# Linear attention with a swish MLP: batches 0 and 1 by head pair, w_in in eight tiles, w_out in 4 KB runs

## The chip, the cores and the metric

The kernel runs on one core of one Trainium2 chip. The metric is the device time of one execution in microseconds, as the median over runs. A profiled execution gives the trace, in which every instruction has a start and a duration. In it PE is TensorE (matmuls; PEld is its weight loads), DVE is VectorE, ACT is ScalarE, POOL is GpSimd, and SP is the engine that only issues DMAs.

## The reference

Inputs q, k, v are float32 of shape (8 batches, 8 heads, 576 positions, 64). The attention is linear: q is softmaxed over the 64 features, k over the 576 positions, and the products are taken as q (k^T v). The result is the input x of a two-layer MLP with 4608 tokens, d_model 512 and d_ff 2048.

```
q_s = exp(q - max(q, -1));  q_s = q_s / (sum(q_s, -1) + 1e-09)
k_s = exp(k - max(k, 2));   k_s = k_s / (sum(k_s, 2) + 1e-09)
kv  = einsum('bhsd,bhse->bhde', k_s, v)
x   = einsum('bhsd,bhde->bhse', q_s, kv)  ->  (B * S, H * D)
h   = x @ w_in
g   = h * (1.0 / (1.0 + exp(-beta * h)))     # beta: one value per d_ff column
out = g @ w_out
```

## The kernel before

**Chunks.** The tokens are cut into nine chunks: the first 512 positions of each of the eight batches, and one chunk (number 8) of the eight tails of 64 positions. They run in the order 0 to 6, 8, 7. For a chunk c, `x_mm` makes the four transposed tiles xT (128 channels, i.e. a pair of heads, by 512 tokens); `mm_a(c, j)` makes the hidden tile h number j of 16 with four matmuls (one per 128 channels, 128x512 each), then ACT's tanh `th` and a DVE multiply `g`; `mm_b(c, j)` adds tile j into the four PSUM accumulators acc0 to acc3 with four matmuls. A block of four such matmuls takes 0.86 us in the chain of the profile. In the steady state blocks of mm_a and mm_b alternate, mm_b two tiles behind mm_a (LAG = 2).

**Attention of a batch.** `q_exp` (ACT), `q_sum` and `q_mul` (DVE) make the softmaxed q, in two halves of four heads. For batches 0 and 1 `q_pet` transposes it on PE, four 128x128 transposes per head pair into a PSUM tile tp, which an engine then copies to qsT. For k only exp is taken; the sum of exp(k) comes from a column of constants beside v. `kv_mm` multiplies exp(k) by v. `kv_norm` divides on DVE by that column and writes the pair's two 64x64 blocks into the diagonal of kvp, with a reciprocal and two multiplies.

**Batches 0 and 1** (b < NW) are special. Their 576 positions are laid over 64 partitions with 9 per partition (RW = 9), and the two heads of a pair stand one above the other on 128 partitions. In the kernel before, exp(k) goes into a zeroed tile in which each head has its own 64 of 128 columns (`kz_exp`, two instructions of 64 partitions for each pair), so that one 128x128 matmul per position makes both heads.

**Order of the work.** The tile framework is in a manual mode: each engine executes its instructions in the order of the code, and waits are semaphores put in from the tiles that instructions share. The whole beginning (batch 0's attention, chunk 0's MLP, batch 1's attention) is therefore written out by hand. `warm` puts dummy matmuls on PE. From chunk 1 on the function `side` places the next batch's work between the blocks.

**Buffers.** PSUM has tags: h with two buffers, att with two, acc0 to acc3 with one each. Weights come in through a staging ring, tag wo, of four buffers of 1 MB; the loads in 2, out 2, in 3 and out 3 wait until the casts of in 0, out 0, in 1 and out 1 have emptied their buffers. The casts to bf16 (`w_cast`) are on POOL but for one.

**DMA queue.** All loads are issued from SP, in the order of the code, and at most eight are under way: each waits for the one eight before it. In the order before: q of batch 0, its four k pairs, its four v pairs, beta, then the weights in the order in 0, out 0 (first half), in 1, out 0 (second half), out 1, in 2, out 2, in 3, then q of batch 1, half of out 3, its k, the other half of out 3, its v, and q, k, v of batch 2.

Of the kernel before, what the change touches and what calls it, by code (L numbers as in the profile page):

```python
# [17 lines left out]
def kernel(  # L18
# [39 lines left out]
    beta_t = const.tile([P, NJ], F32, name="beta_t")  # L58
    beta_r = const.tile([NJ, P], F32, name="beta_r")
    ident16 = const.tile([NJ, NJ], F32, name="ident16")  # L60
    w_in_b = const.tile([P, KT, FF], BF16, name="w_in_b")
    w_out_b = const.tile([P, NJ, DM], BF16, name="w_out_b")
# [9 lines left out]
    w_in_d = moe_w_in.rearrange("(kt p) f -> p kt f", p=P)  # L72
    w_out_d = moe_w_out.rearrange("(j p) f -> p j f", p=P)

# [4 lines left out]

    def load_q(b, parts=1):  # L80
        t = stage.tile([P, H, R * D], F32, tag="q_st", bufs=2, name=f"q_st{b}")
        src = q[b, :, 0:MAIN, :].rearrange("h (p i) d -> p h (i d)", i=R)
        n = H // parts
        for s in range(parts):
            nc.sync.dma_start(t[:, s * n : (s + 1) * n, :], src[:, s * n : (s + 1) * n, :])  # L85
        q_st[b] = t

# [10 lines left out]

    def load_kv(d, src, b, tag, parts=1):
        t = stage.tile([P, H * (R + 1) * D], F32, tag=tag, bufs=2, name=f"{tag}{b}")  # L100
        if b < NW:
            d[b] = t[:, 0 : HP * RW * D].rearrange("p (j r) -> p j r", j=HP)
            sv = src[b].rearrange("(j e) (p i) d -> (e p) j (i d)", e=2, i=RW)
            n = HP // parts
            for s in range(parts):
                nc.sync.dma_start(d[b][:, s * n : (s + 1) * n, :], sv[:, s * n : (s + 1) * n, :])  # L106
        else:
            d[b] = t[:].rearrange("p (h r) -> p h r", h=H)
            nc.sync.dma_start(
                d[b][:, :, 0 : R * D], src[b, :, 0:MAIN, :].rearrange("h (p i) d -> p h (i d)", i=R)  # L110
            )
            e = b % 2
            nc.sync.dma_start(
                d[b][e * TAIL : (e + 1) * TAIL, :, R * D : R * D + D],
                src[b, :, MAIN:S, :].rearrange("h t d -> t h d"),
            )

    def w_load(kind, blk, half=None):
# [3 lines left out]
        if kind == "in":  # L122
            src = w_in_d[:, :, ds(blk * 512, 512)]
            c = slice(0, 512) if half is None else slice(half * 256, half * 256 + 256)
            nc.sync.dma_start(t[:, :, c], src[:, :, c])
        else:
            src = w_out_d[:, ds(4 * blk, 4), :]
            c = slice(0, 4) if half is None else slice(half * 2, half * 2 + 2)
            nc.sync.dma_start(t[:, c, :], src[:, c, :])  # L129

    def w_cast(kind, blk, half, eng):
        t = wst[kind, blk]
        if kind == "in":
            dst = w_in_b[:, :, ds(blk * 512 + half * 256, 256)]
            src = t[:, :, half * 256 : half * 256 + 256]
        else:
            dst = w_out_b[:, ds(4 * blk + 2 * half, 2), :]
            src = t[:, half * 2 : half * 2 + 2, :]
# [7 lines left out]

    def ek_buf(b, eng=None):
        t = work.tile([P, HP * RW * P], BF16, tag="ek", bufs=2, name=f"ek{b}")
        if b < NW:
            ek[b] = t[:].rearrange("p (j i m) -> p j i m", j=HP, i=RW)  # L150
            eng.memset(t[:].bitcast(F32), 0.0)
        else:
            ek[b] = t[:, 0 : R * H * D].rearrange("p (i h d) -> p i h d", i=R, h=H)

    def kz_exp(b, j, m=1):
        for e in range(2):
            r = slice(e * D, (e + 1) * D)
            nc.scalar.activation(  # L158
                ek[b][r, j : j + m, :, e * D : (e + 1) * D],
                k_st[b][r, j : j + m, :].rearrange("p j (i d) -> p j i d", i=RW),  # L160
                ACTF.Exp,
            )

# [63 lines left out]

    def q_mul(b, s, n=2):
        m = H // n
        h = slice(s * m, (s + 1) * m)  # L230
        nc.vector.tensor_tensor(  # L231
            eq[b][:, :, h, :],
# [24 lines left out]
    def kv_mm(b, jj, n=2, tag="att"):  # L257
        t = ps.tile([P, n, D1 if b < NW or COLT else 2 * D1], F32, tag=tag, bufs=2 if tag == "att" else 1, name=f"kv{b}_{jj}")
        att_of[b, jj] = t
        for jl in range(n):  # L260
            j = n * jj + jl
            if b < NW:
                for i in range(RW):
                    nc.tensor.matmul(  # L264
                        t[:, jl, 0:D1],
                        ek[b][:, j, i, :],
                        va[b][:, j, i, :],
                        start=(i == 0),
                        stop=(i == RW - 1),
                    )  # L270
                continue
# [79 lines left out]
    def mm_a(c, j, kts=None, tag=None):  # L351
# [5 lines left out]
        for kt in kts:  # L357
            nc.tensor.matmul(  # L358
                h[:],
                w_in_b[:, kt, ds(j * P, P)],  # L360
                x_of(c)[:, kt, :],
# [115 lines left out]

    load_q(0, parts=2)
    load_kv(k_st, k, 0, "k_st", parts=4)
    load_kv(v_st, v, 0, "v_st", parts=4)  # L480
    nc.sync.dma_start(beta_r[:], moe_beta.rearrange("(j p) -> j p", p=P))
    w_load("in", 0, 0)
    w_load("in", 0, 1)
    w_load("out", 0, 0)
    w_load("in", 1)
    w_load("out", 0, 1)
    w_load("out", 1)
    w_load("in", 2)
    w_load("out", 2)
    w_load("in", 3)  # L490
    load_q(1, parts=2)
    w_load("out", 3, 0)
    load_kv(k_st, k, 1, "k_st", parts=4)
    w_load("out", 3, 1)
    load_kv(v_st, v, 1, "v_st", parts=2)
    load_q(2)
# [4 lines left out]
    make_identity(nc, identity[:])  # L501
    make_identity(nc, ident16[:])
    ek_buf(0, nc.vector)
    nc.vector.memset(kvp[:, 0 : B - 1], 0.0)
    v_buf(0)
    ek_buf(1, nc.gpsimd)
    v_buf(1)

# [14 lines left out]

    warm(18)
    for s in range(2):
        q_exp(0, s)
        q_sum(0, s)
        q_mul(0, s)
    for s in range(2):
        for j in (2 * s, 2 * s + 1):  # L530
            q_pet(0, j, nc.vector)
        warm(10 if s == 0 else 2)
    for j in range(HP):
        kz_exp(0, j)

    tb = ps.tile([P, 512], F32, tag="h", bufs=2, name="tb")

    def attn0(p):
        if 0 < p < 3:
            warm(1, tag="acc3")  # L540
        if p % 2 == 0:
            vz_cast(0, p, nc.gpsimd)
            vz_cast(0, p + 1, nc.gpsimd)
        kv_mm(0, p, n=1, tag=f"acc{p}")
        kv_norm(0, p, n=1)

    for p in range(HP):
        attn0(p)
        if p == 2:
            w_cast("in", 0, 0, nc.gpsimd)  # L550
        if p >= 1:
            x_mm(0, p - 1, nc.scalar)
        if p == 1:
            nc.tensor.transpose(tb[:, 0:NJ], beta_r[:], ident16[:])
            nc.scalar.copy(beta_t[:], tb[:, 0:NJ])
        if p >= 2:
            for j in range(2):
                mm_a(0, j, [p - 2])
    x_mm(0, HP - 1, nc.scalar)
    for kind, blk in (("in", 0), ("out", 0)):  # L560
        for half in range(2):
            if (kind, half) not in (("in", 0), ("out", 1)):
                w_cast(kind, blk, half, nc.gpsimd)
    for kt in (2, 3):
        for j in range(2):
            mm_a(0, j, [kt])
    w_cast("in", 1, 0, nc.vector)
    w_cast("in", 1, 1, nc.gpsimd)
    w_cast("out", 0, 1, nc.gpsimd)
    mm_a(0, 2)  # L570
    mm_a(0, 3)
    mm_b(0, 0)
    mm_b(0, 1)

    def pool_cast(*what):
        for kind, blk in what:
            for half in range(2):
                w_cast(kind, blk, half, nc.gpsimd)

    def tail_zero(t):  # L580
        nc.gpsimd.memset(vt[t][:], 0.0)
        nc.gpsimd.memset(ekt[t][:], 0.0)
        for e in range(2):
            nc.gpsimd.memset(vt[t][ds(e * TAIL, TAIL), e, :, D:D1], 2.0)

    tail_zero(0)
    pool_cast(("out", 1), ("in", 2), ("out", 2))
    tail_zero(1)
    pool_cast(("in", 3), ("out", 3))

    for u in range(4, NJ):
        if u != 5:
            mm_a(0, u)
        if u == 4:
            mm_a(0, 5)
            mm_b(0, 2)
            continue
        if u == 13:
            for j in (0, 1):
                q_pet(1, j, nc.vector)  # L600
        mm_b(0, u - LAG)
        if u in (10, 11):
            q_exp(1, u - 10)
        if u in (10, 12):
            q_sum(1, (u - 10) // 2)
        if u in (11, 13):
            q_mul(1, (u - 11) // 2)
        if u >= 12:
            kz_exp(1, u - 12)
    vz_cast(1, 0, nc.gpsimd, m=2)  # L610
    vz_cast(1, 2, nc.gpsimd, m=2)
    for j in (2, 3):
        q_pet(1, j, nc.vector)
    mm_b(0, NJ - 2)
    kv_mm(1, 0)
    kv_norm(1, 0)
    warm(2)
    kv_mm(1, 1)
    kv_norm(1, 1)
    mm_b(0, NJ - 1)  # L620
    for j in range(HP):
        x_mm(1, j, nc.scalar if j % 2 == 0 else nc.vector, tag="h" if j < 2 else "att")
    for st in range(R):
        store(0, st)
    for kt in range(KT):
        for j in range(2):
            mm_a(1, j, [kt])
    mm_a(1, 2)
    mm_a(1, 3)
# [86 lines left out]
```

The softmax here doesn't subtract the row's maximum and nothing guards it: scores larger than these inputs give would overflow.

## Time and profile before

| | |
|---|---|
| median of 13 runs | 287.96 us (287.62 to 288.41) |
| the profiled execution | 287.74 us, its span 286.0 us |
| PE busy | 279.3 us (98%) |
| DVE, ACT, POOL busy | 180.4, 162.8, 43.7 us |
| h matmuls (line 358), 128x512 | 576, 379 ns each from start to end |
| acc matmuls (line 399), 128x512 | 560, 379 ns each |
| th on ACT (line 368) / g on DVE (line 370) | 687 / 682 ns each |
| first half of batch 0's q arrives, exp starts | 4.56 us |
| first h matmul | 15.33 us |
| x of chunk 1 / its first h matmul | 47.87 / 48.92 us |

The span runs from the first to the last instruction; the time of the execution is 1.74 us longer. [...] the next one starts 216 ns after it (four in 0.86 us). In the first 48 us the DMA engines are 90% busy or more and move 330 to 400 GB/s; later they have room.

### The profile page before, as it was taken

How to read it: one execution, taken by the hardware profiler on the slowest of the kernel's cores; microseconds unless marked ns; L12 is line 12 of the kernel's file. 1: busy time of each engine (PE TensorE's matmuls, PEld its weight loads, DVE VectorE, ACT ScalarE, POOL GpSimd, SP SyncE). 2: the span in 40 equal slices, each digit the busy share in tenths (PEclk: the TensorE clock that was granted, in tenths of full speed). 3: DMA queues.
4: the chain of work that ended last, by engine and by line, in shares of the span. 5: the costliest groups of instructions: out<-in, count | busy, mean ns of one | idle time of the engine just before them, and what ended most of it. 6: DMA issues, size and time to landing. Idle time of an engine off the chain costs nothing.

```text
span 286.0 us, 4169 instructions
## 1 busy us (share of the span) xinstructions
PE 279.3 (98%) x1611; PEld 129.8 (45%) x1611; DVE 180.4 (63%) x281; ACT 162.8 (57%) x236; POOL 43.7 (15%) x58
## 2 busy tenths in 40 slices
PE   8899999999999999999999999999999999999995
PEld 3444445444444444444444444444445444445543
DVE  7944497695478457854694569546964596455361
ACT  4763586684486448734683468355934564554451
POOL 4458833210030030000300030003000000000000
PEclk9999999999999999999999999999999999999999
DMA  7999999908942963197219912793370033005003
GB/s 231 381 382 388 370 389 326 290 5 247 293 155 65 322 168 143 28 328 202 93 56 252 300 42 109 176 268 109 147 197 25 1 149 73 0 0 149 0 0 147
DMA packets 56371, 50.08 MB, mean 175 GB/s; under 512 B 26256, under 2 KB 48032, under 8 KB 56352
## 3 DMA queue, kind: packets, MB, share of 16 engines
q1 hardware_dynamic: 56208, 49.69, 56.2%
q8 instruction: 12, 0.20, 0.3%
q10 hardware_dynamic: 144, 0.13, 0.1%
q14 instruction: 7, 0.06, 0.1%
HBM read 36.71 MB, written 9.44 MB: 161 GB/s over the span
## 4 chain that ended last, share of the span: by engine, by line
PE 85%; DMA 11%; SPq 1%; POOL 1%; issue 0%; ACT 0%; ACTq 0%
PE h L358 40%; PE acc L399 39%; DMA w_in<-in_moe_w_in_dram 6%; DMA k_st<-in_k_dram 5%; PE x L314 2%; PE kv L276 2%; PE acc L391 1%; POOL w_in_b L145 1%; PE kv L264 0%; PE tp L250 0%; SPq L85 0%; SPq L106 0%; PE x L318 0%; ACT ek L158 0%; SPq L129 0%
## 5 line engine op out<-in xcount | busy, mean ns | idle before, releaser
L368 ACT ACTIVATE th<-h,beta_t 128x512 bf16<-128x512 f32 x144 | 98.6, 687 | 99.0 <-PE h L358 97.2
L370 DVE SCALAR_TENSOR_TENSOR g<-th,h 128x512 bf16<-128x512 bf16 x144 | 97.9, 682 | 88.7 <-ACT th L368 87.3
L358 PE MATMUL h<-xT,w_in_b 128*128 128x512 bf16 x576 | 145.3, 379 | 0.6 <-POOL w_in_b L145 0.3
L399 PE MATMUL acc<-w_out_b,g 128*128 128x512 bf16 x560 | 141.9, 379 | 0.0
L358 PEld LDWEIGHTS <-w_in_b 128*128 128x128 bf16 x576 | 55.3, 98 | 66.3 <-issue 2.7
L399 PEld LDWEIGHTS <-g 128*128 128x128 bf16 x560 | 54.5, 98 | 65.5 <-DVE g L370 0.5
L145 POOL CAST va<-v_st 128x2048 bf16<-128x2048 f32 (+2 forms) x12 | 17.2, 1456 | 144.5 <-DMA v_st<-in_v_dram 144.5
L225 DVE TENSOR_REDUCE rq<-eq 128x16 f32<-128x1024 bf16 x18 | 21.6, 1198 | 2.5 <-ACT eq L214 2.5
L231 DVE TENSOR_TENSOR eq<-eq,rq 128x1024 bf16<-128x1024 bf16 x18 | 22.6, 1254 | 0.1
L214 ACT ACTIVATE eq<-q_st 128x1024 bf16<-128x1024 f32 x16 | 16.3, 1048 | 3.0 <-DMA q_st<-in_q_dram 2.9
L143 ACT CAST xT<-x 128x512 bf16<-128x512 f32 x20 | 11.6, 586 | 10.9 <-PE x L314 10.1
L145 DVE COPY o<-acc 128x512 f32<-128x512 f32 (+1 forms) x19 | 12.1, 670 | 3.4 <-PE acc L399 3.2
L143 ACT COPY o<-acc 128x512 f32<-128x512 f32 (+1 forms) x18 | 9.5, 578 | 5.8 <-PE acc L399 2.9
L169 ACT ACTIVATE ek<-k_st 128x1024 bf16<-128x1024 f32 x12 | 12.6, 1047 | 0.0
L472 PE MATMUL warm<-kvp 128*128 128x512 bf16 x34 | 11.2, 480 | 1.2 <-DVE kvp L500 1.2
L314 PE MATMUL x<-qsT,kvp 128*128 128x512 bf16 x32 | 11.7, 380 | 0.4 <-DVE kvp L309 0.2
L158 ACT ACTIVATE ek<-k_st 64x576 bf16<-64x576 f32 x16 | 10.9, 679 | 0.8 <-DMA k_st<-in_k_dram 0.6
L145 DVE CAST xT<-x 128x512 bf16<-128x512 f32 x16 | 10.9, 684 | 0.5 <-PE x L314 0.5
L145 POOL CAST w_out_b<-w_out 128x1024 bf16<-128x1024 f32 x8 | 8.2, 1042 | 6.7 <-DMA w_out<-in_moe_w_out_dram 6.5
L309 DVE TENSOR_TENSOR kvp<-kv,rk 64x256 bf16<-64x256 f32 (+2 forms) x24 | 8.0, 333 | 0.6
L145 POOL CAST w_in_b<-w_in 128x1024 bf16<-128x1024 f32 x7 | 7.2, 1042 | 3.6 <-DMA w_in<-in_moe_w_in_dram 3.5
L472 PEld LDWEIGHTS <-kvp 128*128 128x128 bf16 x34 | 3.8, 119 | 6.2 <-issue 3.8
(40 smaller groups left out, 75.3 us busy)
## 6 DMA issues: line engine op xcount, KB each, us to landing
out_dram<-o SPq DMA_DIRECT2D x14, 512.0 KB, 3.4
q_st<-in_q_dram SPq DMA_DIRECT2D x6, 1024.0 KB, 6.6
k_st<-in_k_dram SPq DMA_DIRECT2D x6, 1024.0 KB, 9.1
v_st<-in_v_dram SPq DMA_DIRECT2D x6, 1024.0 KB, 10.6
w_in<-in_moe_w_in_dram SPq DMA_DIRECT2D x3, 1024.0 KB, 9.8
k_st<-in_k_dram SPq DMA_DIRECT2D x8, 288.0 KB, 7.6
q_st<-in_q_dram SPq DMA_DIRECT2D x4, 512.0 KB, 7.8
w_out<-in_moe_w_out_dram SPq DMA_DIRECT2D x4, 512.0 KB, 9.5
```

What stands on the lines that cost most here:

```text
L143: eng.copy(dst, src)
L145: eng.tensor_copy(dst, src)
L169: nc.scalar.activation(ek[b][:, :, h, :].rearrange("p i h d -> p h i d"), k_st[b][:, h, 0 : R * D].rearrange("p h (i d) -> p h i d", i=R), ...
L214: nc.scalar.activation(eq[b][:, :, s * m : (s + 1) * m, :].rearrange("p i h d -> p h i d"), q_st[b][:, s * m : (s + 1) * m, :].rearrange(" ...
L225: nc.vector.tensor_reduce(rq[b][:, 0, :, h], eq[b][:, :, h, :], axis=AX.X, op=ALU.add)
L231: nc.vector.tensor_tensor(eq[b][:, :, h, :], eq[b][:, :, h, :], rq[b][:, 1, :, h].unsqueeze(3).to_broadcast((P, R, m, D)), ALU.mult,)
L314: nc.tensor.matmul(t[:], kvp[:, c, j, :], qsT[c][:, :, j, :])
L358: nc.tensor.matmul(h[:], w_in_b[:, kt, ds(j * P, P)], x_of(c)[:, kt, :], start=(kt == 0), stop=(kt == KT - 1),)
L368: nc.scalar.activation(th[:], h[:], ACTF.Tanh, scale=beta_t[:, j : j + 1])
L370: nc.vector.scalar_tensor_tensor(out=g[:], in0=th[:], scalar=1.0, in1=h[:], op0=ALU.add, op1=ALU.mult)
L399: nc.tensor.matmul(acc[st][:], g[:, ds(st * P, P)], w_out_b[:, j, :], start=(j == 0), stop=(j == NJ - 1),)
L472: nc.tensor.matmul(t[:, 0:cols], kvp[:, B - 1, 0, :], kvp[:, B - 1, :, :].rearrange("p j r -> p (j r)")[:, 0:cols],)
```

## The change

- **exp(k) dense.** For batches 0 and 1 exp(k) goes into a tile without zeros, one instruction of 128x576 for each pair. The zeroing of the two ek tiles is gone.
- **kv in quadrants.** Each 128x128 matmul becomes two of 64x64, one for each head, at tile positions (0, 0) and (64, 64).
- **By head pair.** k and v of both batches are loaded pair by pair, k and v in turn. exp, the cast of v, kv_mm and kv_norm run pair by pair too; three of the four qsT copies of batch 0, and one of batch 1's, move to ACT.
- **w_in in eight tiles.** w_in_b becomes eight tiles of 256 columns. Hidden tile j now is every second column of tile j // 2, so a weight load reads with a step of two elements. beta is read as 8 rows of 256 and transposed in two steps to match.
- **w_out in 4 KB runs.** A partition takes two neighbouring rows of w_out (4 KB), where it took rows of 2 KB from different places.
- **Order.** The last weight block (out 3) is loaded behind k and v of batch 1. In chunk 0, mm_b(0, 0..3) stand together, and mm_b(0, 12..15), which use out 3, stand behind x and the first two h tiles of chunk 1. One half of in 1 is cast on ACT instead of DVE.

The core of the diff:

```diff
-    w_in_b = const.tile([P, KT, FF], BF16, name="w_in_b")
+    w_in_b = [const.tile([P, KT, 2 * P], BF16, name=f"w_in_b{hh}") for hh in range(NJ // 2)]
...
-    w_out_d = moe_w_out.rearrange("(j p) f -> p j f", p=P)
+    w_out_d = moe_w_out.rearrange("(hh p e) f -> p hh e f", p=P, e=2)
+    w_in_u = [t[:].rearrange("p kt (q e) -> p kt e q", e=2) for t in w_in_b]
...
+    def kz_exp(b, j):
+        if j == 0:
+            ek_buf(b)
+        nc.scalar.activation(ek[b][:, j, :], k_st[b][:, j, :], ACTF.Exp)
...
+                    for e in range(2):
+                        r = slice(e * D, (e + 1) * D)
+                        nc.tensor.matmul(
+                            t[r, jl, 0:D1],
+                            ek[b][r, j, ds(i * D, D)],
+                            va[b][r, j, i, :],
+                            start=(i == 0),
+                            stop=(i == RW - 1),
+                            tile_position=(e * D, e * D),
+                        )
...
-                w_in_b[:, kt, ds(j * P, P)],
+                w_in_u[j // 2][:, kt, j % 2, :],
...
+    load_q(0, 2)
+    for j in range(HP):
+        load_kv(k_st, k, 0, "k_st", [j])
+        load_kv(v_st, v, 0, "v_st", [j])
     w_load("in", 0, 0)
+    nc.sync.dma_start(beta_r[:], moe_beta.rearrange("(hh q) -> hh q", q=2 * P))
     w_load("in", 0, 1)
     w_load("out", 0, 0)
+    w_load("out", 0, 1)
     w_load("in", 1)
-    w_load("out", 0, 1)
     w_load("out", 1)
     w_load("in", 2)
     w_load("out", 2)
+    load_q(1, 2, 0)
     w_load("in", 3)
...
+    load_q(1, 2, 1)
+    for j in range(HP):
+        load_kv(k_st, k, 1, "k_st", [j])
+        load_kv(v_st, v, 1, "v_st", [j])
+    w_load("out", 3)
...
+    warm(18)
+    q_exp(0, 0)
+    q_sum(0, 0)
+    q_mul(0, 0)
+    q_exp(0, 1)
+    kz_exp(0, 0)
+    vz_cast(0, 0, nc.gpsimd)
+    q_sum(0, 1)
+    q_mul(0, 1)
+    kz_exp(0, 1)
+    vz_cast(0, 1, nc.gpsimd)
+    warm(5)
+    q_pet(0, 0, nc.scalar)
+    q_pet(0, 1, nc.scalar)
+    kv_mm(0, 0, n=1, tag="acc0")
+    kv_norm(0, 0, n=1)
+    warm(3)
+    kv_mm(0, 1, n=1, tag="acc1")
+    kv_norm(0, 1, n=1)
+    kz_exp(0, 2)
+    vz_cast(0, 2, nc.gpsimd)
+    q_pet(0, 2, nc.scalar)
+    q_pet(0, 3, nc.vector)
+    kz_exp(0, 3)
+    vz_cast(0, 3, nc.gpsimd)
+    x_mm(0, 0, nc.scalar, tag="h")
+    warm(1, tag="acc0")
+    kv_mm(0, 2, n=1, tag="acc2")
+    kv_norm(0, 2, n=1)
+    x_mm(0, 1, nc.scalar, tag="h")
+    warm(3, tag="acc1")
+    x_mm(0, 2, nc.scalar)
+    kv_mm(0, 3, n=1, tag="acc3")
+    kv_norm(0, 3, n=1)
...
+    for kt in range(KT):
+        for j in range(2):
+            mm_a(0, j, [kt])
+    mm_a(0, 2)
+    mm_a(0, 3)
+    for j in range(4):
+        mm_b(0, j)
+    w_cast("in", 1, 0, nc.scalar)
...
+    for u in range(6, NJ - 2):
+        mm_a(0, u, tag="att" if u == 6 else None)
+        if u == 9:
+            q_exp(1, 0)
+            q_sum(1, 0)
+        if u == 10:
+            q_mul(1, 0)
+        if u == 12:
+            q_exp(1, 1)
+            q_sum(1, 1)
...
+            q_mul(1, 1)
+            kz_exp(1, 0)
+        mm_b(0, u - 2)
+    q_pet(1, 0, nc.vector)
+    q_pet(1, 1, nc.vector)
+    mm_a(0, NJ - 2)
+    kv_mm(1, 0, n=1)
+    kz_exp(1, 1)
+    mm_a(0, NJ - 1)
+    kv_norm(1, 0, n=1)
+    kv_mm(1, 1, n=1)
+    kv_norm(1, 1, n=1)
+    kz_exp(1, 2)
+    q_pet(1, 2, nc.scalar)
+    q_pet(1, 3, nc.vector)
+    kz_exp(1, 3)
+    x_mm(1, 0, nc.scalar, tag="h")
+    kv_mm(1, 2, n=1)
+    kv_norm(1, 2, n=1)
+    x_mm(1, 1, nc.vector, tag="h")
+    kv_mm(1, 3, n=1)
+    kv_norm(1, 3, n=1)
+    x_mm(1, 2, nc.scalar)
+    x_mm(1, 3, nc.scalar)
     for kt in range(KT):
         for j in range(2):
             mm_a(1, j, [kt])
+    for j in range(NJ - 4, NJ):
+        mm_b(0, j)
+    for st in range(R):
+        store(0, st)
```

In the changed kernel's order of instructions DVE stands thus around batch 1: the second q_sum, g13, the second q_mul, the copies of tp(1,0) and tp(1,1), g14, g15, the norms of pairs 0 and 1, the copy of tp(1,3), the norm of pair 2, the copy of x(1,1), the norm of pair 3.

## The prediction

> **What bounds the kernel now.** The page first: PE is busy 98% of the span and the granted clock is 9 tenths or more in every slice, so outside a few holes nothing but PE time counts (that row does not show everything: the first warm matmuls start 0.43 us apart until 6.7 us, later ones 0.216).
>
> ```profile
> span 286.0 us, 4169 instructions
> PE 279.3 (98%) x1611; PEld 129.8 (45%) x1611; DVE 180.4 (63%) x281; ACT 162.8 (57%) x236; POOL 43.7 (15%) x58
> PE 85%; DMA 11%; SPq 1%; POOL 1%; issue 0%; ACT 0%; ACTq 0%
> ```
>
> The chain that ended last gives 85% to PE and 11% to DMA. Its answer for the first 52 us shows where DMA stands in it: only ahead of 39 us.
>
> ```profile
> 8.91 6.79 DMA w_in<-in_moe_w_in_dram
> ...
> 16.83 10.26 DMA w_in<-in_moe_w_in_dram
> ...
> 28.68 8.94 DMA k_st<-in_k_dram
> ...
> 39.19 0.61 PE tp L250 x8
> ...
> 48.92 3.29 PE h L358 x14
> ```
>
> From 48.92 on, PE is dense to the end. So the change, which touches only batches 0 and 1, is worth what it does to one moment: when the third h tile of chunk 1 starts (mm_a(1,2)). Before, 8 matmuls at 0.216 us (four in 0.86, chain) follow 48.92, so that is **50.65 us**. The timeline of that stretch has the holes and the durations for the sum:
>
> ```profile
> 37.17 1.88 DVE L231 TENSOR_TENSOR eq<-eq,rq 128x1024 bf16<-128x1024 bf16 x1
> ...
> 39.19 0.61 PE L250 MATMUL tp<-identity,eq 128*128 128x128 bf16 x8 [0.70 <-ACT ek L158]
> ...
> 41.52 0.74 DVE L145 COPY qsT<-tp 128x512 bf16<-128x512 bf16 x2
> ...
> 45.42 0.74 PE L264 MATMUL kv<-va,ek 128*128 128x65 bf16 x18
> ...
> 47.01 1.02 PE L399 MATMUL acc<-w_out_b,g 128*128 128x512 bf16 x4
> ```
>
> The copies of the transposes start 1.7 us after these end, and PE does not notice: in between it has mm_b and mm_a blocks.
>
> [...] the multiply above took 1.88 us, the other multiplies that I looked up 1.21 to 1.23; it began 0.25 us after a POOL cast (36.92 to 37.96). [...] about 0.1 us on each side of the 64-column kv block at 66.39 to 67.03. [...]
>
> **Start, to h(0,2) (before: 18.04 + 2 x 0.216 = 18.47).** Removed at no gain: the ek memsets (DVE 1.98, POOL 2.11); DVE then waits for q's exp until 5.65 anyway, POOL for v until 10.45. exp(k) falls from 8 half-partition instructions in 5.58 us (7.44 to 13.02) to 4 of 0.68 (same free size of 576). Landings, from k0 at 7.40 (1.34 MB asked for up to there) and v0 at 10.40 (2.52 MB): 0.393 MB/us, so v pairs land at 8.15, 9.65, 11.15, 12.65 and k pairs 0.75 earlier. The second q multiply becomes ready at 9.87, POOL holds a v cast from 9.7: I let it lose 0.5 (bounds 0 and 0.66), ending 11.6. On DVE follow norms of pairs 0 and 1 (0.17 + 0.46 each), a qsT copy 0.42, so pair 2's norm ends 14.1, x_mm(0,2) is done 14.4, kv pair 3 starts 14.5, its norm ends 15.65, x_mm(0,3) starts 15.7. Eight h matmuls follow; their xT (ACT 0.59) is done 16.7, in time. h(0,2) starts **17.65** (17.15 without the lock): 0.8 earlier. The two small beta transposes (0.23 each) and beta's DMA lie beside pair 3's norm; fewer warm matmuls (30 for 34) matter only there.
>
> **Chunk 0 up to mm_b(0,11).** DMA takes part of this back. Delivered bytes at a landing exceed the asked-for sum by 0.43 MB up to 20 us, by 0.63 MB from 27 (windows of the DMA rate against the casts). In the new order w_in 1 is at 6.55 MB, lands 21.3; ACT's cast (estimate 1.04, as POOL's) ends 22.4; it is needed six blocks of 0.864 (four matmuls) after 17.65, at 22.84. w_out 1 lands 24.3, cast 25.4, needed three blocks later, 25.43. w_in 2 lands 27.07, cast by 28.16, so mm_a(0,8) starts **28.22** (before 28.83) whether the start gained 0.8 or 1.3. w_out 2 lands 29.8, needed 32.5; w_in 3 lands 34.0, cast 35.1, needed 35.13. Eight blocks of 0.86 later mm_b(0,11) ends at **38.6**. The 4 KB runs may quicken w_out: 1 KB runs moved at 358 GB/s, 2 KB at 388, 2.3 KB at 396; 4 KB could give 0 to 5% on 3.1 MB, 0 to 0.4 us; I take 0. Separate w_in tiles cost nothing: the casts stay 1.04 and are hidden by PE. SP issues 2 more DMAs for v of batch 1 (0.45 each) while MBs are queued ahead; moving w_out 3 behind them brings the last v pair from about 44 to 41.6 and w_out 3 from 41.3 to 44.4, harmless as it is used after 50.
>
> **The hand-over to batch 1 (the loss).** Before, mm_b(0,12..15) stood among transposes, kv and x. Now 16 mm_b matmuls (3.46 us) stand behind x, and these waits have no cover. PSUM tag att has two buffers, which tp0, tp1, kv0, kv1, tp2, tp3, kv2, kv3 take in turn; the changed program's list of waits shows kv(1,0) waiting for the DVE copy of tp(1,0).
> - mm_a(0,12) ends 36.0, th12 (0.69) 36.85, second q exp (1.05) 37.9, reduce (1.21) and reciprocal (0.25) 39.45, g13 (0.68) 40.15, second multiply (1.22, or 0.55 more behind a POOL v cast at 40.05; I take half) 41.65, copy of tp0 (0.42) 42.1. PE has meanwhile done both transposes (0.44) and mm_a(0,14) and stands since 39.93: **2.2 us idle**.
> - kv(1,0) 0.4 with its mode changes, mm_a(0,15) to 43.4, kv(1,1) to 43.8. tp(1,2) needs kv(1,0)'s buffer, freed by its norm, which on DVE stands behind g15: th15 44.3, g15 45.0, norm 45.7. PE starts tp(1,2) at 45.75: **1.95 idle**.
> - From there a serial chain: norm of pair 1 and tp(1,3) 0.9, x(1,0); ACT's copy frees the buffer for kv(1,2), done +1.7; norm, copy of x(1,1) (0.68) and norm of pair 3 on DVE, +3.8; x(1,3) ends +4.05: 49.8. PE has 2.2 us of work in it.
> - 8 h matmuls (1.73) and the 16 postponed mm_b (3.46): mm_a(1,2) at **55.0**. The output copies (ACT 0.59, DVE 0.68, two each) run beside mm_a(1,2), (1,3), 1.73 us: hidden.
>
> Kv in quadrants: 18 matmuls for 9 per pair. The 64-column kv had 40 in 0.64, 16 ns each; if quadrants pair up likewise a pair still takes 0.29, if not 0.58, at most 0.3 x 4 in the hand-over. I take the first.
>
> **Sum.** 55.0 - 50.65 = +4.3 on the profiled execution's 287.74 us (span 286.0 and 1.74 around it): 292.0. The median of 13 is 287.96, 0.2 above that execution, so **292.2**. Bounds: lock costs -0.5/+0.5, w_out's runs -0.4, unpaired quadrants +1.2, my waits 0.5 either way: 290.9 to 294.
>
> **Unknown prices.** A half clock after the two holes: [...] PE works only about a third of 39.9 to 49.8. Lower bound 0 (no hole can gain); upper, the next 16 matmuls at double time, +3.5. I take 0. Weights at step 2 (w_in): loads take 98 ns and start a full matmul ahead, so even doubled they fit into 216 ns: 0; upper bound if some fail to, 10 ns each x 576 = +5.8. [...]
>
> **Rivals.**
> - Main: the waits, 292.2; chance 0.70. For it: the waits are in the program, the durations in the trace. Against: it needs DVE's order to bind at each link.
> - Half clock in the hand-over: 292.2 plus 1 to 3.5, 293.2 to 295.7; 0.10. Against: matmuls kept 0.216 through the thin PE work at 12 to 18 us, though warm matmuls helped there.
> - Strided weights tell: above 295; 0.05.
> - The hand-over costs little and w_out runs help: 288.6 to 290.9; 0.05.
> - **Faster**, the other side: the early exp, v casts and loads of batch 1 keep DVE ahead, and PE stays dense there. From 28.22 the dense work is mm_a(0,8..15) 6.9, mm_b(0,6..15) 8.6, transposes 0.9, kv 1.6, x 0.9, h(1,0..1) 1.7 = 20.6, so 48.85: 1.8 better, 286.2. It decides where the idle of the hand-over (6.1 by my count) stays below 1.8. 0.07, with 286.2 to 287.4. The gain of the start alone, 0.6 at 28.22, is what speaks for it.
> - Within 0.2% (0.58 us, about what a measurement can tell): 0.03.
>
> Slower is 0.70 + 0.10 + 0.05 + 0.05 = 0.90. The range 290.3 to 295.7 holds the main case, the half clock and a little of the milder one, 0.82.
>
> **What would show it.** Right: h(0,2) near 17.6; mm_a(0,8) near 28.2 behind a POOL cast; PE waits of about 2 us ended by a DVE copy of a transpose and by a norm (line 312), x(1,3) near 49.6, then 24 matmuls, and from there the old chain 4 us later. Wrong: no PE hole over 1 us between 39 and 50; matmuls 0.43 apart after it; or h matmuls more than 0.216 apart in later chunks.

## Result and the profile after

The changed kernel takes **293.4 us** in the median (291.38 to 294.24, 11 runs) against 288.02 (48 runs of the kernel before beside it): ratio 1.0171, 95% interval 1.0156 to 1.0187. It is slower, and the range forecast holds it; but it lies 1.2 above the 292.2 that was taken as likeliest, and the reason for that difference is one of the prediction's rivals, the half clock. The profiled execution took 293.72 us, with a span of 291.9 (before: 287.74 and 286.0).

The page of the changed kernel, span and busy line, clock row of the 40 slices, and the chain by engine:

```profile
span 291.9 us, 4299 instructions
PE 282.0 (97%) x1680; PEld 130.5 (45%) x1680; DVE 176.5 (60%) x280; ACT 160.7 (55%) x234; POOL 43.7 (15%) x60
PEclk9999996899999999999999999999999999999999
PE 90%; DVE 5%; ACT 2%; DMA 1%; issue 0%
```

The share of DMA in the chain fell from 11% to 1%, and DVE, which had none worth naming, has 5%. The clock row has two slices, the seventh and eighth (44 to 58 us), where the granted clock is below nine tenths.

The timeline of the hand-over, that is, of the stretch from the last tiles of chunk 0 to the third h tile of chunk 1, in which batch 1's attention is made (start us, duration, engine, line, operation; in brackets the idle time before and who ended it):

```profile
38.50 0.61 PE L250 MATMUL tp<-identity,eq 128*128 128x128 bf16 x8
38.95 1.03 PE L361 MATMUL h<-xT,w_in_b 128*128 128x512 bf16 x4
...
39.75 1.21 DVE L231 TENSOR_TENSOR eq<-eq,rq 128x1024 bf16<-128x1024 bf16 x1
...
40.88 0.75 DVE L150 COPY qsT<-tp 128x512 bf16<-128x512 bf16 x2
...
41.44 0.48 PE L266 MATMUL kv<-va,ek 64*64 64x65 bf16 x18 [1.47 <-DVE qsT L150]
...
43.65 0.69 DVE L373 SCALAR_TENSOR_TENSOR g<-th,h 128x512 bf16<-128x512 bf16 x1 [1.43 <-ACT th L371]
...
44.45 0.46 DVE L312 TENSOR_TENSOR kvp<-kv,rk 64x64 bf16<-64x64 f32 x2
...
44.96 0.40 PE L250 MATMUL tp<-identity,eq 128*128 128x128 bf16 x4 [1.67 <-DVE kvp L312]
...
49.06 0.59 PE L317 MATMUL x<-qsT,kvp 128*128 128x512 bf16 x1 [0.67 <-ACT xT L148]
...
49.44 3.62 PE L361 MATMUL h<-xT,w_in_b 128*128 128x512 bf16 x8
...
52.85 3.88 PE L402 MATMUL acc<-w_out_b,g 128*128 128x512 bf16 x16
...
56.57 1.67 PE L361 MATMUL h<-xT,w_in_b 128*128 128x512 bf16 x7
```

Both holes (idle stretches of PE) are there with the releasers forecast: a copy of a transpose behind the second q multiply, and a norm behind g15. Then come the x matmuls and 24 dense matmuls. mm_a(1,2) starts at 56.57 where it had been 50.65: 5.92 later, and the span is 5.9 longer, so nothing behind it adds to the loss. What was not in the main case stands in the line at 49.44: eight h matmuls take 3.41 us up to 52.85, 0.43 each. The windows of 1 us (busy us of PE, PEld, DVE, ACT, POOL, then granted clock, DMA share, GB/s) show why:

```profile
44.00:45.00 1.00, 0.04 (x1) 0.04 (x2) 0.92 (x5) 0.19 (x1) 1.00 (x2) 1.00 1.10 349
...
46.00:47.00 1.00, 1.00 (x21) 0.47 (x19) 0.68 (x3) 1.00 (x2) 1.00 (x2) 0.77 1.09 348
47.00:48.00 1.00, 1.00 (x20) 0.67 (x19) 0.95 (x3) 0.04 (x1) 0.79 (x4) 0.50 1.18 330
...
52.00:53.00 1.00, 1.00 (x4) 0.45 (x3) 0.00 (x0) 0.33 (x1) 0.00 (x0) 0.50 1.09 250
53.00:54.00 1.00, 1.00 (x6) 0.37 (x5) 0.61 (x2) 0.94 (x2) 0.00 (x0) 0.81 0.25 55
```

The windows from 47 to 53 all have 0.50; 0.77 and 0.81 at the two ends mean that the clock was at half from 46.54 to 53.38, 6.84 us (an estimate: 0.46 and 0.38 of these two windows at 0.50). It is so in some executions only. The 12 executions of the changed kernel, by mean granted clock: seven at 0.988 took 293.4 to 294.24 (mean 293.9), one at 0.994 took 292.3, four at 1.000 took 291.38 to 292.23 (mean 291.8). So the half clock costs 2.1 us, and the median is that of a mixture. Below, "whole clock" means executions at 0.998 or above.

### The profile page after: what moved, and what is told of

It reads as the page before. It is cut to its first block, busy times and chain, and to the rows that moved or that the text cites. A ratio compares the mean times of both kernels' runs of the same rounds, so it can differ in the third digit from the quotient of the medians.

```text
span 291.9 us, 4299 instructions
## 1 busy us (share of the span) xinstructions
PE 282.0 (97%) x1680; PEld 130.5 (45%) x1680; DVE 176.5 (60%) x280; ACT 160.7 (55%) x234; POOL 43.7 (15%) x60
## 4 chain that ended last, share of the span: by engine, by line
PE 90%; DVE 5%; ACT 2%; DMA 1%; issue 0%
PE h L361 42%; PE acc L402 40%; PE x L317 3%; DVE eq L231 2%; DVE rq L225 2%; PE kv L279 2%; DMA q_st<-in_q_dram 1%; PE acc L394 1%; ACT eq L214 1%; DVE g L373 1%; PE kv L266 1%; DVE kvp L312 0%; PE warm L475 0%; DVE rq L226 0%; PE tp L250 0%
## 5 line engine op out<-in xcount | busy, mean ns | idle before, releaser
L150 POOL CAST va<-v_st 128x576 bf16<-128x576 f32 (+1 forms) x14 | 18.1, 1298 | 152.3 <-DMA v_st<-in_v_dram 152.3
L148 ACT CAST xT<-x 128x512 bf16<-128x512 f32 x21 | 12.2, 586 | 9.2 <-PE x L317 8.4
L317 PE MATMUL x<-qsT,kvp 128*128 128x512 bf16 x32 | 12.8, 401 | 1.1 <-ACT xT L148 0.7
L475 PE MATMUL warm<-kvp 128*128 128x512 bf16 x30 | 9.6, 465 | 1.3 <-DVE kvp L505 1.2
L150 DVE CAST xT<-x 128x512 bf16<-128x512 f32 x15 | 10.3, 684 | 0.0
L312 DVE TENSOR_TENSOR kvp<-kv,rk 64x64 bf16<-64x64 f32 (+1 forms) x28 | 8.6, 308 | 0.7
L150 POOL CAST w_in_b<-w_in 128x1024 bf16<-128x1024 f32 (+1 forms) x8 | 8.3, 1060 | 4.1 <-DMA w_in<-in_moe_w_in_dram 4.1
L162 ACT ACTIVATE ek<-k_st 128x576 bf16<-128x576 f32 x8 | 5.4, 680 | 1.1 <-DMA k_st<-in_k_dram 1.1
```

The lines of the kernel that those rows point to most:

```text
L148: eng.copy(dst, src)
L150: eng.tensor_copy(dst, src)
L317: nc.tensor.matmul(t[:], kvp[:, c, j, :], qsT[c][:, :, j, :])
L475: nc.tensor.matmul(t[:, 0:cols], kvp[:, B - 1, 0, :], kvp[:, B - 1, :, :].rearrange("p j r -> p (j r)")[:, 0:cols],)
```

## Experiments

**1. Copies of the first transposes on ACT.** It takes the DVE copies out of the first hole.

```
-    q_pet(1, 0, nc.vector)
-    q_pet(1, 1, nc.vector)
+    q_pet(1, 0, nc.scalar)
+    q_pet(1, 1, nc.scalar)
```

> The copies of tp(1,0) and tp(1,1) go to ACT instead of DVE. Theory (each idle stretch of PE is a wait in a chain of DVE work, and the stretches add up): kv(1,0) no longer stands behind the second q multiply on DVE, so it starts at about 39.8 in place of 41.44; DVE is 0.75 us freer, so kv(1,0)'s norm and with it tp(1,2) come about 1.4 earlier (43.6 in place of 44.96), and everything behind x(1,3) too: 290.4 where the clock stays whole, 292.5 where it halves. Rival 1 (only the second hole counts, since it waits for g15 on DVE whatever kv(1,0) does): the first hole shrinks, tp(1,2) stays within 0.4 of 44.96, and the time stays within 0.5 of the changed kernel's. Rival 2 (ACT is the next bound: its copies push th14 and th15 back): tp(1,2) later than 45.3 and a time above 294.

Measured: 291.7 in the median of 4, ratio 1.0126 (1.0072 to 1.018); by clock 289.74 at 1.000, 290.92 at 0.994, 292.48 and 293.56 at 0.988, so there is one execution at whole clock. Its timeline:

```profile
39.90 0.48 PE L266 MATMUL kv<-va,ek 64*64 64x65 bf16 x18
...
43.41 0.40 PE L250 MATMUL tp<-identity,eq 128*128 128x128 bf16 x4 [1.62 <-DVE kvp L312]
```

kv(1,0) has no hole ahead of it and starts 1.54 earlier, tp(1,2) 1.55 earlier. A hole of 1.62 still stands ahead of tp(1,2), so the first hole was added to the second, not hidden in it. Both rivals fall.

**2. Both first norms ahead of g15.**

```
-    mm_a(0, NJ - 1)
     kv_norm(1, 0, n=1)
     kv_mm(1, 1, n=1)
     kv_norm(1, 1, n=1)
     kz_exp(1, 2)
+    mm_a(0, NJ - 1)
```

> In the hand-over, kv(1,1), the norms of kv(1,0) and kv(1,1) and the exp of pair 2 are issued ahead of mm_a(0,15), so that DVE does both norms before g15. Theory (the second hole is the norm standing behind g15): first hole unchanged (kv(1,0) at 41.4), tp(1,2) at about 43.2 in place of 44.96, x(1,3) 1.4 to 1.7 earlier, 290.2 at whole clock, 292.4 with a half one. Rival (x(1,1) to x(1,3) hang on the DVE chain, which holds the same work in either order): tp(1,2) is early but x(1,3) stays within 0.4 of 49.06, the time within 0.4 of the changed kernel's.

Measured: 290.0, ratio 1.0076 (1.0049 to 1.0103); 289.57, 289.66 and 290.33 at whole clock, 291.39 at 0.992. Its timeline:

```profile
41.45 0.81 PE L266 MATMUL kv<-va,ek 64*64 64x65 bf16 x36 [1.46 <-DVE qsT L150]
42.19 1.04 PE L361 MATMUL h<-xT,w_in_b 128*128 128x512 bf16 x4
43.06 0.88 PE L250 MATMUL tp<-identity,eq 128*128 128x128 bf16 x8
```

The first hole is unchanged and the second is gone: transposes follow mm_a(0,15) at 43.06, with 43.2 expected. So the second hole came from g15 standing ahead of the norm in DVE's order (the norm of pair 0 now starts at 42.34, in the changed kernel at 44.45). The edit also puts mm_a(0,15) behind kv(1,1) on PE, where it runs while DVE does the norms.

**3. Two postponed blocks put into the chain.** mm_b(0,12) ahead of kv(1,3), mm_b(0,13) ahead of x(1,3).

```
     x_mm(1, 1, nc.vector, tag="h")
+    mm_b(0, NJ - 4)
     kv_mm(1, 3, n=1)
     kv_norm(1, 3, n=1)
     x_mm(1, 2, nc.scalar)
+    mm_b(0, NJ - 3)
     x_mm(1, 3, nc.scalar)
...
-    for j in range(NJ - 4, NJ):
+    for j in range(NJ - 2, NJ):
         mm_b(0, j)
```

> Of the four postponed blocks mm_b(0,12..15), 12 goes between x(1,1) and kv(1,3) and 13 between x(1,2) and x(1,3); 14 and 15 stay where they were. Theory (PE has 2.2 us of work in the 4.1 us from tp(1,2) to x(1,3), so postponed work put there costs less than its length): 0.9 to 1.4 us less than the changed kernel, 290.4 to 290.9 at whole clock; the two idle stretches at 40 and 44 stay. PE is also busier in the 6 us ahead of the h block, so if thin work halves the clock, it does so more seldom or for less time. Rival (the chain x(1,1), kv(1,3), x(1,2) has no slack and each block put in delays it by its whole 0.86): the same time as the changed kernel within 0.4. Second rival (w_out's last block, cast late, holds the two blocks up): slower by up to 1.

Measured: 290.56, ratio 1.0079 (1.0053 to 1.0105); two executions at whole clock, both 289.85; 291.27 at 0.994 and 292.26 at 0.988. The gain at whole clock, 291.8 - 289.85 = 1.95, is above the 0.9 to 1.4 expected; the spread of the changed kernel's own times at whole clock (0.85) covers the difference. Two of four executions still lose clock, and the profiled one shows it behind the first hole already, in its windows:

```profile
42.00:43.00 1.00, 1.00 (x20) 0.53 (x15) 0.59 (x1) 0.00 (x0) 0.00 (x0) 0.75 1.08 367
...
49.00:50.00 1.00, 0.85 (x7) 0.32 (x8) 0.69 (x1) 0.00 (x0) 0.00 (x0) 0.83 1.10 234
```

By the same reckoning, from 42.50 to 49.34: again 6.84 us.

**4. Extra matmuls in both holes of PE.** `pad(t, n)` puts n matmuls of 128x512 into tile t.

```
     mm_a(0, NJ - 2)
+    h_of[0, NJ - 1] = ps.tile([P, MAIN], F32, tag="h", bufs=2, name="h0_15")
+    pad(h_of[0, NJ - 1], 6)
     kv_mm(1, 0, n=1)
...
     kz_exp(1, 2)
+    x10 = ps.tile([P, MAIN], F32, tag="h", bufs=2, name="x1_0")
+    pad(x10, 7)
     q_pet(1, 2, nc.scalar)
```

> Extra matmuls, whose results are overwritten, are put into the two idle stretches of PE in the hand-over: six of 128x512 ahead of kv(1,0), seven ahead of tp(1,2). Every wait of the real work stays. Half-clock theory (the matmuls at 0.43 us after x(1,3) come from too little PE work over the 10 us before): all executions show h(1,0..1) in about 1.73 us in place of 3.41 and mm_a(1,2) at about 54.5 in place of 56.57; the times gather at 291.4 to 292.2, like the quicker executions of the changed kernel, and none at 293.4 to 294.3. Rival (the half clock is set off by something else, as a jump in load when dense work comes back): as many executions at 293.4 and above as of the changed kernel. Rival 2 (the h matmuls are slow for another reason, as strided weights or SBUF traffic): 3.41 us stays in all.

Measured: 291.9 (291.12 to 292.3, 4 runs), ratio 1.0131 (1.0113 to 1.0148), clock 0.999 or 1.000 in all four. Its timeline:

```profile
49.99 1.68 PE L366 MATMUL h<-xT,w_in_b 128*128 128x512 bf16 x7
51.50 3.62 PE L407 MATMUL acc<-w_out_b,g 128*128 128x512 bf16 x16
54.95 1.89 PE L366 MATMUL h<-xT,w_in_b 128*128 128x512 bf16 x8
```

The first line has seven of the eight h matmuls (one record is missing); from it to the next line they take 1.51, 0.216 each, and mm_a(1,2) starts at 54.95. Waits as before, more work for PE, and a kernel faster by 1.5 in the median: the slow matmuls go with the clock (0.43 apart where it was 0.50, 0.216 here), and rival 2, which had them slow in all executions, falls.

**5. Extra matmuls in the second hole only.** As 4, without the six ahead of kv(1,0).

> The changed kernel with extra matmuls (results overwritten) in the second idle stretch only, seven of 128x512 ahead of tp(1,2); the first, of 1.5 to 1.8 us ahead of kv(1,0), stays. All waits of the real work stay. Theory A (the clock falls when PE's work over some 6 to 10 us is thin, and both holes count together): 1.000 in nearly all executions, times at 291.2 to 292.4. Theory B (one hole of 1.5 us or more can start it by itself): clock 0.988 in about half of the executions, with times near 293.5 to 294, and the slow matmuls begin at 42 to 43, behind the first hole.

Measured: 291.57 (291.37 to 291.7, 4 runs), ratio 1.0108 (1.0079 to 1.0137), clock 0.999 or 1.000 in all four, with the first hole still there:

```profile
41.79 0.48 PE L266 MATMUL kv<-va,ek 64*64 64x65 bf16 x18 [1.47 <-DVE qsT L150]
```

So that hole alone did not do it in four executions. Together 4 and 5 have 8 of 8 at whole clock, the changed kernel 4 of 12. Four executions of each are few. Runs 1 to 4 were on one chip, where runs 1 to 3 lost clock in 6 of 12 executions and run 4 in none of 4; run 5 was on another chip.

**6. The kernel before, with mm_b(0,12..15) and the stores of chunk 0 postponed and nothing else.**

```
-        mm_b(0, u - LAG)
+        if u < NJ - 2:
+            mm_b(0, u - LAG)
...
-    mm_b(0, NJ - 2)
     kv_mm(1, 0)
...
-    mm_b(0, NJ - 1)
     for j in range(HP):
...
             mm_a(1, j, [kt])
+    for j in range(NJ - 4, NJ):
+        mm_b(0, j)
+    for st in range(R):
+        store(0, st)
```

> The kernel before with only one thing of the new order: mm_b(0,12..15) and the stores of chunk 0 are put behind the h matmuls of h(1,0) and h(1,1); pairs, exp and kv stay as before. Theory (postponed blocks are cover taken from the hand-over, whatever way kv is made): tp(1,2) then waits for the second q multiply (ends 43.4 on DVE), kv(1,0) for the copies (about 45.1), x(1,3) ends at 48.4 to 48.9, 8 h and 16 mm_b matmuls follow (5.2 us): mm_a(1,2) at 53.6 to 54.1, so 290.9 to 291.4 at whole clock, up to 2.2 more where it halves. Rival (the loss belongs to kv by pair, with its att buffers taken in turn, and not to the postponement): within 0.5 of the kernel before.

Measured: 291.07 (290.69 to 291.75, 4 runs), ratio 1.0108 (1.0095 to 1.0122); three at whole clock, one at 0.994. Its timeline:

```profile
44.13 0.61 PE L250 MATMUL tp<-identity,eq 128*128 128x128 bf16 x8 [0.88 <-ACT ek L158]
45.99 0.74 PE L264 MATMUL kv<-va,ek 128*128 128x65 bf16 x18 [1.25 <-DVE qsT L145]
...
50.86 3.62 PE L399 MATMUL acc<-w_out_b,g 128*128 128x512 bf16 x16
54.31 1.89 PE L358 MATMUL h<-xT,w_in_b 128*128 128x512 bf16 x8
```

+3.0 us without any kv by pair: holes ahead of transposes and kv where mm_b had been, and mm_a(1,2) 3.66 later in the profiled execution (291.33, 0.26 above the median). The postponement alone is enough for the greater part of the loss. The +3.8 of the changed kernel at whole clock is net of its earlier start, so the stretch from mm_a(0,8) to mm_a(1,2) compares them better: it takes 21.8 in the kernel before, 54.31 - 29.10 = 25.2 here, and 56.57 - 28.08 = 28.5 in the changed kernel, about 26.4 without the 2.1 of half clock. So 3.4 of about 4.6 come with the postponement. The other 1.2 would belong to the rest of the new order (exp, kv and norms by pair); no run takes that alone.

**7. The kernel before, with only the layout of the weights changed** (eight w_in tiles, step 2 in their loads, w_out in 4 KB runs, beta in two transposes).

```
-    w_in_b = const.tile([P, KT, FF], BF16, name="w_in_b")
+    w_in_b = [const.tile([P, KT, 2 * P], BF16, name=f"w_in_b{hh}") for hh in range(NJ // 2)]
...
-    w_out_d = moe_w_out.rearrange("(j p) f -> p j f", p=P)
+    w_out_d = moe_w_out.rearrange("(hh p e) f -> p hh e f", p=P, e=2)
+    w_in_u = [t[:].rearrange("p kt (q e) -> p kt e q", e=2) for t in w_in_b]
...
-                w_in_b[:, kt, ds(j * P, P)],
+                w_in_u[j // 2][:, kt, j % 2, :],
```

> The kernel before with only the layout of the weights changed: eight tiles of w_in, step 2 in its weight loads, w_out in 4 KB runs in the place of its old order, beta in two transposes; order of all work as before. Theory (the layout costs PE nothing and DMA is off the path at those moments): 287.7 to 288.3, weight loads of w_in at 98 ns. Rival 1 (strided loads are slower and show at a rate of one in 0.216 us): above 289, up to 293.8, h matmuls further apart than 0.216. Rival 2 (4 KB runs bring w_in 2 earlier): 287.4 to 287.7, mm_a(0,8) earlier than 28.83 by 0.2 to 0.5.

Measured: 287.38 (287.18 to 288.32, 13 runs) beside 288.11, ratio 0.9985 (0.9976 to 0.9994). Groups of lines (busy, mean ns of one), then its timeline:

```profile
L359 PE MATMUL h<-xT,w_in_b 128*128 128x512 bf16 x558 | 143.9, 379 | 1.6 <-POOL w_in_b L146 0.3 <-ACT xT L144 0.2
L359 PEld LDWEIGHTS <-w_in_b 128*128 128x128 bf16 x576 | 55.4, 98 | 66.2 <-issue 2.7 <-POOL w_in_b L146 0.6
```

```profile
36.36 1.04 POOL L146 CAST w_out_b<-w_out 128x1024 bf16<-128x1024 f32 x1 [1.28 <-DMA w_out<-in_moe_w_out_dram]
...
37.07 1.40 DVE L232 TENSOR_TENSOR eq<-eq,rq 128x1024 bf16<-128x1024 bf16 x1
```

Weight loads of w_in stay at 98 ns and their matmuls at 379: a step of 2 costs nothing here. The time falls by 0.15% in the ratio and by 0.73 us (0.25%) in the medians, near the 0.2% that the prediction calls measurable; the interval leaves out no change. It is not mm_a(0,8) that moves (28.92, before 28.83), so rival 2 has its size but not its place. The two profiles differ in one: on POOL the cast of the first half of w_out's last block starts 0.56 earlier (before at 36.92), overlaps the first q multiply of batch 1 by 0.33 in place of 0.79, and that multiply takes 1.40 in place of 1.88; the transposes follow 0.57 earlier (38.62). That the longer runs bring the cast forward is not shown: in run 6's profile, whose loads are those of the kernel before, the transposes start at 39.76, 0.57 behind the 39.19 of before, so two profiles of the same loads differ by as much.

**8. Edits 1 to 3 together.** The diff is the three above.

> The three edits of the hand-over together: copies of tp(1,0), tp(1,1) on ACT, both first norms ahead of g15, and postponed blocks 12 and 13 of mm_b inside the chain. Theory (the loss is idle time of PE in the hand-over, 6.1 us of it in the changed kernel over a dense floor at which mm_a(1,2) would start at 48.85): the first hole goes, since kv(1,0) follows mm_a(0,14) at 39.9; tp(1,2) follows mm_a(0,15) at about 41.7; the 0.9 hole ahead of x(1,3) takes mm_b(0,13). 0.5 to 1.5 us of idle stay, mm_a(1,2) at 49.4 to 50.3, so 286.7 to 287.6: below the kernel before, by what the quicker start is worth. Clock whole in all executions. Rival (the gains overlap, since one and the same DVE chain sets x(1,3) in all of them): no better than the best of the three alone, 289.6 to 290.

Measured: 288.88 (288.27 to 289.74, 7 runs), ratio 1.0032 (1.0021 to 1.0044), whole clock in all. Worth 2.9 over the changed kernel at whole clock; alone the three gave about 2 each (run 1 by a single execution at whole clock), so they overlap, but less than the rival had it. The theory's 286.7 to 287.6 was missed: what was filled left three other waits, in its timeline:

```profile
41.47 0.48 PE L266 MATMUL kv<-va,ek 64*64 64x65 bf16 x18 [0.94 <-ACT ek L162]
...
44.17 0.48 PE L266 MATMUL kv<-va,ek 64*64 64x65 bf16 x18 [0.53 <-ACT qsT L148]
...
45.53 1.02 PE L402 MATMUL acc<-w_out_b,g 128*128 128x512 bf16 x3 [0.56 <-POOL w_out_b L150]
```

ACT, which took the copies, is late with exp of pair 1; and mm_b(0,12), which fills a hole, needs w_out's last block, whose load the change had put behind k and v.

**9. Another order of the hand-over.** Only blocks whose weights are long there serve as fill; norms come before gates on DVE, copies before gates on ACT. The hand-over's order, its calls for PE alone:

```
mm_a(0,12)  mm_a(0,13)  tp(1,0)  tp(1,1)  mm_b(0,10)  mm_a(0,14)  kv(1,0)
half of mm_b(0,11)  kv(1,1)  mm_a(0,15)  tp(1,2)  tp(1,3)  x(1,0)  kv(1,2)
half of mm_b(0,11)  kv(1,3)  x(1,1)  x(1,2)  mm_b(0,12)  x(1,3)  h(1,0..1)  mm_b(0,13..15)
```

> The changed kernel with its hand-over in another order, all else as it is: mm_b(0,10) and mm_b(0,11), whose w_out block is long there, are kept for the hand-over (11 in two halves, around kv(1,1) and kv(1,2)); exp of k pair 1 comes ahead of th14; on DVE both first norms come ahead of g14, on ACT the copy of tp(1,2) ahead of th15; tp(1,0) and tp(1,1) are copied on ACT; mm_b(0,12) stands ahead of x(1,3). Theory (idle of PE in the hand-over is the whole loss; in the version with three edits together 0.94 of it waited for exp of pair 1, 0.53 for a copy on ACT, 0.56 for the cast of w_out's last block): transposes at about 37.8, kv(1,1) at 40.6 to 41.0, tp(1,2) at 41.9 to 42.2, x(1,3) done by 47.3, mm_a(1,2) at 49.0 to 49.9, so 286.3 to 287.3, which would be 0.7 to 1.7 under the kernel before. Rival (DVE and ACT need the time until 47 whatever the order, so PE's blocks end up idle elsewhere): 288 to 289, as the three edits together.

Measured: 288.53 (287.87 to 289.22, 14 runs), ratio 1.0006 (0.9992 to 1.002), whole clock in all: the rival. Its timeline:

```profile
35.02 2.10 DVE L231 TENSOR_TENSOR eq<-eq,rq 128x1024 bf16<-128x1024 bf16 x1
...
37.77 1.02 PE L361 MATMUL h<-xT,w_in_b 128*128 128x512 bf16 x4 [1.25 <-DVE g L384]
```

With mm_b(0,10) taken away from behind mm_a(0,12), the next h tile waits for g11, and g11 for a multiply of 2.10 that ran beside POOL's cast of w_in. But the expectation was also wrong in its sum: x(1,3), expected done by 47.3, starts at 47.55 and ends 0.22 later, and the 20 matmuls behind it take 4.3. Even its own 47.3 would have given mm_a(1,2) at 51.6, not 49.0 to 49.9; it came at 52.08.

**10. A second order.** mm_b(0,10) back at its place, half of w_in's last block cast on ACT, the second q exp and sum ahead of th12, exp of pairs 2 and 3 earlier.

```
         if u == 10:
             q_mul(1, 0)
+            w_cast("in", 3, 0, nc.scalar)
+        if u == 11:
+            q_exp(1, 1)
+            q_sum(1, 1)
         if u == 12:
-            q_exp(1, 1)
-            q_sum(1, 1)
+            kz_exp(1, 0)
+            q_mul(1, 1)
```

> A second order of the hand-over, from what the first showed (mm_a(0,13) stood 1.25 us behind g11, which was behind a first q multiply of 2.10 beside a POOL cast of w_in; kv(1,3) stood 0.64 behind an exp): half of w_in's last block is cast on ACT, so that POOL is done with it when the multiply starts; the second q exp and its sum are issued a step earlier, ahead of th12; mm_b(0,10) is back at its place; exp of pairs 2 and 3 come ahead on ACT. Theory: first multiply 1.2 to 1.4, kv(1,0) at 40.0, tp(1,2) at 41.6 to 42, x(1,3) done at 44.7 to 46, mm_a(1,2) at 49.3 to 50.0, so 286.4 to 287.3, 0.7 to 1.6 under the kernel before, clock whole. Rival (the new order moves a hole elsewhere again): 287.6 to 288.6, level with the kernel before.

Measured: 288.27 (287.76 to 288.61, 13 runs), ratio 1.0006 (0.9998 to 1.0015), whole clock in all. Its timeline:

```profile
45.63 0.39 PE L317 MATMUL x<-qsT,kvp 128*128 128x512 bf16 x1 [0.35 <-DVE kvp L312]
...
51.31 1.89 PE L361 MATMUL h<-xT,w_in_b 128*128 128x512 bf16 x7
```

The steps came (first multiply 1.45, kv(1,0) at 40.04, x(1,3) started at 45.63), but mm_a(1,2) is at 51.31, with 49.3 to 50.0 expected. Again the expected sum did not follow from its steps: with x(1,3) done at 44.7 to 46, the 24 matmuls behind it (5.2 us) lead to 49.9 to 51.2. From mm_a(0,8) on it takes 51.31 - 28.59 = 22.7 us, the kernel before 50.65 - 28.83 = 21.8. The 20.6 of dense work are about the same, so it still has 2.1 of idle time in many small waits, and the start of this execution is only 0.24 ahead. No order tried here is under the kernel before; the layout alone (7) is, by 0.15% in the ratio.

## Why the prediction was right, and what was mis-sized

- **Start: right.** The h block starts at 15.92, so h(0,2) at 15.92 + 8 x 0.216 = 17.65, as forecast. That it is exact is in part luck, as two errors cancel. The delay of the second multiply beside POOL's v cast, which the prediction calls the lock, was over-sized (1.38 in the chain, where 1.22 + 0.5 was taken, from the 1.88 of before), so the norm of pair 2 ended at 13.62 and not at 14.1; but x_mm(0,2) still started only at 14.15, behind three warm matmuls. In the profile of run 9, whose beginning is the same, the block starts at 16.50 although this multiply took 1.22, so the start moves by half a microsecond for other reasons than this delay. An exp(k) of a whole pair, 128x576, takes 0.680 in the changed kernel, where the 64x576 of before took 0.679: 0.68 had been taken.
- **Chunk 0: right.** mm_a(0,8) at 28.08 (28.22), mm_b(0,11) ends at 38.50 (38.6): the gain is 0.82 at h(0,2) and 0.75 at mm_a(0,8), behind a POOL cast. The prediction's "Eight blocks of 0.86 later" is a slip of the count: 38.6 lies four blocks behind 35.13, twelve behind 28.22.
- **First hole: right in cause, too long.** 1.47 for 2.2. The multiply took 1.21 (1.22 and 0.27, half of the 0.55 that a v cast might cost, had been taken) and q's exp came 0.15 earlier. The remaining 0.3 is DVE's: several of its instructions start up to 0.1 before the one ahead has ended (the copy at 40.88, the multiply until 40.96), and the sum had set them end to end.
- **Second hole: right.** 1.67 for 1.95, behind g15, as run 2 shows. tp(1,2) at 44.96 (45.75).
- **Chain from tp(1,2) to the end of x(1,3): right.** 4.05 forecast; 44.96 to 49.44 is 4.48, with part of it at half clock; at whole clock, in run 4, x(1,3) starts at 49.55 and ends 0.22 later, 3.98 after tp(1,2) at 45.79.
- **Sum at whole clock: right.** 292.2 forecast, 291.8 measured over four executions, 291.57 and 291.9 in runs 5 and 4. The two holes together were 1.0 shorter than forecast, so the sum agrees better than its terms; the four executions spread over 0.85. The bounds as listed add up to 290.8 and 294.4, where 290.9 and 294 were written.
- **Half clock: the term that was mis-sized.** Taken as 0 with bounds of 0 and +3.5 (an estimate: 16 matmuls at the 0.43 us of the first warm ones in place of 0.216); it measured 2.1 and came in seven of twelve executions, so the median is in the rival's 293.2 to 295.7, to which I had given a chance of 0.10. The step that failed was to take 0, an estimate of mine that no trace of before could bear out: the longest hole in its hand-over is 0.70. Here the longest was 1.67, and the clock fell to 0.50. Thin matmuls at 12 to 18 us had kept their pace of 0.216 and were taken as evidence against; warm matmuls stood among them, and runs 4 and 5, which put such matmuls in, keep the clock too (0.999 or 1.000). In the kernel before the first matmuls stand 0.43 us apart from 1.19 to 6.7 us, which is 5.5 us, with 1.00 in the clock column of the windows there; the reason is not shown.
- **Layout of the weights: right for the loads** (0: 98 ns each in run 7 as before; the 10 ns of the upper bound was an estimate of mine, with no trace behind it), and the 4 KB runs' "0 to 0.4" stays open: run 7 is faster by 0.4 in the ratio, but its profile does not show that the runs did it.
- **Quadrants pair up: right.** 18 kv matmuls leave PE free after 0.41 (39.90 to 40.31 in run 1), where 0.29 (at 16 ns each) and 0.1 had been taken. That 0.1, for what the prediction calls mode changes, is the gap of about 0.1 us on each side of the 64-column kv block of before. Unpaired, at the 32 ns of a 128*128 kv matmul of before (18 in 0.58 in its chain), it would have been 0.58 and 0.1.
- **The faster rival fell** where it said it would decide: the holes alone are 3.1, above 1.8. Run 10 has 2.1 of idle time left and comes level, not lower.

## What to carry to other kernels

A block of matmuls that stands in the middle of a dependency chain is cover; before postponing it, go through the chain's waits and ask what PE has left to do in each (here 3.46 us moved out, 3.0 lost, with only the stores moved along). When holes are closed one by one, the next late thing is on the engine that took the work over: three edits worth 2 us each alone gave 2.9 together. And after a thin stretch of PE look at the granted clock (here 0.50 for 6.84 us) in windows of 1 us, and at the clocks of all executions, not at one profile.

## What was not expected of the hardware

- The clock fell to half (0.50) for 6.84 us, the same length in the two profiles that caught it, with no hole longer than 1.83. It began at 46.54 in one and at 42.50 in the other, and only in some executions of the same program. Executions with a mean clock of 0.994 fit a stay of about half that length (an estimate: 0.006 x 290 us / 0.5 = 3.5 us). What sets it off stays open. With the second hole filled it stayed whole (8 of 8); with the first taken away (run 1) it did not (2 of 4 at 0.988, one at 0.994). PE's busy share from 40 to 46 us does not order them: by the windows it is 0.68 in run 1's profile, where three of four executions lost clock, and 0.65 in run 8's, where none of seven did. And the kernel before, whose longest hole in the hand-over is 0.70 in its profile, lost clock too, in one of the 64 executions beside the experiments (290.15 at 0.994).
- DVE's multiply of q takes longer beside a POOL cast, and the more so the longer they overlap, where the cast began first: 1.21 alone, 1.40 with 0.33 of overlap (run 7), 1.45 with 0.38 and 1.58 with 0.51 (run 10), 1.88 with 0.79 (before), 2.10 with 1.02 (run 9). Each is the overlap longer, less some 0.13. Where the multiply began first, the casts took longer: in the changed kernel it took 1.21 from 39.75 on, and the two casts begun at 39.85 took 2.25 together, where the one before them took 0.67.
